# Half of a weight slab's load moved from SyncE's queue to ScalarE's, behind a dummy matmul

## The chip, the core and the metric

The kernel runs on one core of a Trainium2 chip. The core has five engines with queues of their own: TensorE (PE; its weight loads are listed as PEld), ScalarE (ACT), VectorE (DVE), GpSimd (POOL) and SyncE (SP). SP and ACT also issue DMAs, which move data between the chip's memory (HBM) and the core's SBUF. The metric is the device time of one execution in microseconds (us); lower is better.

## The reference

The kernel computes a two-layer block with a Silu between:

```
B, S, D, F = 1, 2048, 640, 1728
h = einsum("bsd,df->bsf", x, w1)
h = silu(h)
out = einsum("bsf,fd->bsd", h, w2)
```

All inputs and the output are bf16: x is 2048x640, w1 is 640x1728, w2 is 1728x640.

## The kernel before, in words

The first product is computed with the F dimension on the partitions. D is cut into five slices of 128 (the index k), F into 13 tiles of 128 (ft) and a rest of 64, S into four chunks of 512 (c). A matmul takes a 128x128 piece of w1 as weights and 512 columns of the transposed x as moving data, and five of them, one for each k, accumulate one tile of h in a PSUM bank. ACT applies Silu from the bank into `hT` (line 193). Then the second product runs from `hT` and `w2s`, results are copied out by DVE and ACT (lines 253 and 255), and SP stores them.

The first chunk's first eight ft tiles are computed in another order, so that PE can begin before all of w1 is there. `k_pass(k)` (lines 197 to 204) runs the eight matmuls of one k into eight banks, and five passes follow one another (lines 206 to 210). Pass k needs slab k, the 1024 columns of w1 that belong to k (256 KB, loaded by `load_k`, line 125), and two or one k slices of the transposed x (three DMA transposes, line 120, by `first(i)`: k 0 and 1, then 2 and 3, then 4). Slab 0 is loaded in two halves of 512 columns (128 KB): the first is needed by the matmuls of ft 0 to 3, the second by those of ft 4 to 7. Line 200 makes PE wait for the second half before ft 4.

The order of the DMAs is written out by hand, and a queue issues its DMAs one after another. The helper `ahead_of_start` puts an instruction ahead of the engine's part in the start barrier; `barrier_wait_here` moves an engine's wait for that barrier to the current place in its queue. The barrier opens when the Drain of each engine has been passed, and ACT, DVE, POOL and PE then go on. On SP, ahead of the Drain, stand: the transpose for k 0 and 1, the second half of slab 0 (line 149), slab 1, the transpose for k 2 and 3, slab 2 and slab 3. Behind it come the transpose for k 4, slab 4, the two groups of the other w1 columns (line 158), SP's wait for the barrier, the nine transposes of the other chunks and the loads of w2. On ACT, ahead of its Drain, stands the first half of slab 0 (line 147); behind the barrier come a wait for POOL's memset of `warm`, the load of the Silu table, one small activation (line 165) and then the Silus.

PE begins with 14 dummy matmuls on a zeroed tile `z` (128x256, line 183), which need only DVE's memset (line 138). They write bank 3, whose contents the first real matmul on it overwrites. Then come the passes, and PE's wait for the barrier stands after pass 1. `tick` attaches a semaphore increment to an instruction; `wait` makes an engine wait for a value, once.

Of the kernel before, what the change touches and what calls it, by code (L numbers as in the profile page):

```python
# [9 lines left out]
def bass_standalone__dense_activation_silu__prompt_kernel(  # L10
# [13 lines left out]
    P = 128  # L24
    NB = 8
# [5 lines left out]
    HB = 256  # L31
# [6 lines left out]
    pe, act, dve, pool, sp = nc.tensor, nc.scalar, nc.vector, nc.gpsimd, nc.sync  # L38

    with ExitStack() as es:  # L40
        def sb(name, shape, dtype):
            return es.enter_context(nc.sbuf_tensor(name, shape, dtype))

        xT = sb("xT", [P, DT, S], bf16)
        w1s = sb("w1s", [P, DT, F], bf16)
# [7 lines left out]
        z = sb("z", [P, HB], bf16)  # L53
        ps = es.enter_context(nc.psum_tensor("ps", [P, NB, BANK], fp32))
# [4 lines left out]
        def sem(name):  # L59
            s = es.enter_context(nc.semaphore(name))  # L60
            count[s.name if hasattr(s, "name") else name] = 0
            return [s, 0]

        def tick(ins, s, n=1):
            ins.then_inc(s[0], n)
            s[1] += n
            return (s, s[1])

        def wait(eng, *points):
            for pt in points:  # L70
                if pt is None:
                    continue
                s, v = pt
                key = (id(eng), id(s))
                if seen.get(key, 0) < v:
                    eng.wait_ge(s[0], v)
                    seen[key] = v

        s_pe, s_act, s_dve = sem("s_pe"), sem("s_act"), sem("s_dve")
# [4 lines left out]
        def load(eng, out_ap, in_ap):  # L84
            s = sem(f"s_ld{n_dma[0]}")
            n_dma[0] += 1
            return tick(eng.dma_start(out=out_ap, in_=in_ap), s, 16)

        ET = mybir.EngineType

        def preamble(engine, opcode):
            lst = nc.main_func.blocks[0].instructions
            return next(
                i for i, ins in enumerate(lst)
                if ins.opcode == opcode and ins.engine == engine
            )

        def ahead_of_start(emit, engine):
            lst = nc.main_func.blocks[0].instructions
            n = len(lst)  # L100
            r = emit()
            lst = nc.main_func.blocks[0].instructions
            new = lst[n:]
            del lst[n:]
            at = preamble(engine, "Drain")
            lst[at:at] = new
            return r

        def barrier_wait_here(engine):
            lst = nc.main_func.blocks[0].instructions  # L110
            lst.append(lst.pop(preamble(engine, "EventSemaphore")))

        w1_v = w1.rearrange("(dt p) f -> p dt f", p=P)
        w2_v = w2[0:F0, :].rearrange("(ft p) d -> p ft d", p=P)

        FA = 8
# [16 lines left out]
        def first(i):  # L133
            k0, k1 = KT[i]
            pt = turned(0, k0, k1, s_x[i])
            for k in range(k0, k1):
                ld_x[k] = pt
        p_z = ahead_of_start(lambda: tick(dve.memset(z[:, :], 0.0), s_dve), ET.DVE)  # L138
        FH = FA // 2
        ld_k = {}  # L140

        def slab(k):
            ld_k[k] = load_k(sp, k)

        ahead_of_start(lambda: first(0), ET.SP)
        ld_k0a = ahead_of_start(
            lambda: load(act, w1s[:, 0, 0:FH * P], w1_v[:, 0, 0:FH * P]), ET.Activation)
        ld_k[0] = ahead_of_start(
            lambda: load(sp, w1s[:, 0, FH * P:FA * P], w1_v[:, 0, FH * P:FA * P]), ET.SP)
        ahead_of_start(lambda: slab(1), ET.SP)  # L150
        ahead_of_start(lambda: first(1), ET.SP)
        ahead_of_start(lambda: slab(2), ET.SP)
# [3 lines left out]
        for a, b in FG:  # L156
            e = F if b == FT else b * P
            pt = load(sp, w1s[:, :, a * P:e], w1_v[:, :, a * P:e])
            for ft in range(a, b):
                ld_w1[ft] = pt  # L160
        barrier_wait_here(ET.SP)

        p_warm = tick(pool.memset(warm[:, :], 0.0), s_pool)  # L163
        wait(act, p_warm)
# [10 lines left out]
            load(sp, w2t[0:FL, :], w2[F0:F, :]),  # L175
            load(sp, w2t[FL:2 * FL, :], w2[F0:F, :]),
        ]

        bank_free = [None] * NB

        def dummies(n):
            for _ in range(n):
                pe.matmul(ps[:, 3, 0:HB], lhsT=z[:, 0:P], rhs=z[:, :], start=True, stop=True)  # L183

        wait(pe, p_z)
        dummies(14)

        def mm(o, l, r, start, stop, shared=False):
            return pe.matmul(o, lhsT=l, rhs=r, start=start, stop=stop, skip_group_check=shared)  # L189
# [7 lines left out]
        def k_pass(k):  # L197
            for ft in range(FA):
                if k == 0 and ft == FH:
                    wait(pe, ld_k[0])  # L200
# [19 lines left out]
        for ft in range(FA, FT):  # L220
            wait(pe, ld_w1[ft])
            b = bank()
            for k in range(DT):
                ins = mm(ps[:, b, :], w1s[:, k, ft * P:(ft + 1) * P], xT[:, k, 0:SCH],
                         start=(k == 0), stop=(k == DT - 1))
            silu(hT[:, ft, 0:SCH], ps[:, b, :], b, tick(ins, s_pe))
        for c in range(1, NSC):
            wait(pe, ld_xc[c])
            for ft in range(FT):
                b = bank()  # L230
                for k in range(DT):
                    ins = mm(ps[:, b, :], w1s[:, k, ft * P:(ft + 1) * P],
                             xT[:, k, c * SCH:(c + 1) * SCH], start=(k == 0), stop=(k == DT - 1))
                h_last = silu(hT[:, ft, c * SCH:(c + 1) * SCH], ps[:, b, :], b, tick(ins, s_pe))
        h_tail = []
        for q in range(NSC // 2):
            b = bank()
            for k in range(DT):
                for hh in range(2):
                    c = 2 * q + hh  # L240
                    ins = mm(ps[hh * FL:(hh + 1) * FL, b, :], w1s[:, k, F0:F],
                             xT[:, k, c * SCH:(c + 1) * SCH],
                             start=(k == 0), stop=(k == DT - 1), shared=True)
# [82 lines left out]
        for c in range(NSC):  # L326
            b = bank()
            wbank.append(b)
            for ft in range(FT):
                mm(ps[:, b, :], w2s[:, ft, DA:D], hT[:, ft, c * SCH:(c + 1) * SCH],  # L330
                   start=(ft == 0), stop=False)
# [51 lines left out]
```

## Time and profile before

| what | us |
|---|---|
| median of 5 runs | 124.95 |
| lowest and highest run | 124.69, 125.12 |
| the profiled execution | 124.77 |
| its span, first to last instruction | 123.4 |
| PE busy | 121.1 |
| ACT busy | 38.1 |
| DVE busy | 7.5 |
| the first half of slab 0 (ACT), issue to landing | 2.2 |
| the second half of slab 0 (SP), issue to landing | 3.2 |
| the transposes of x, median issue to landing | 4.0 |

The span starts with the first instruction that the profile has, SP's first transpose. In a line of the timeline the first number is the start, the second the duration, then come the engine, the line of the kernel, the operation and its tiles, and xN says how many instructions were merged. A q behind the engine's name marks its queue: a DMA's line there is the time of its issue, not of its transfer. Brackets give the idle time before it and what ended it. PEld overlaps PE, so an idle PEld is no loss in itself. Ends of matmuls are modelled; starts are what their pace is read from.

### The profile page before, as it was taken

Reading aid. Unit: us, or ns where it says so; the run is one execution under the profiler, and the core shown is the slowest. Engines: PE = TensorE matmul, PEld = TensorE weight load, DVE = VectorE, ACT = ScalarE, POOL = GpSimd, SP = SyncE. Lnnn points to the kernel's source line nnn. Section 1 sums busy time; section 2 is a strip of 40 time slices with the busy share of each in tenths; the row PEclk is TensorE's granted clock in tenths of the full one; section 3 lists DMA queues with packets and bytes.
Section 4 is the critical chain, followed back from the end, with each engine's and each line's share of the span. In section 5 each row is a group of like instructions: output and inputs, shape, how many; then the busy total and the mean of one; then the engine's idle time right before and its main releaser. Section 6 shows DMA issues by size and latency. Waiting matters only on the chain.

```text
span 123.4 us, 1342 instructions
## 1 busy us (share of the span) xinstructions
PE 121.1 (98%) x588; PEld 55.2 (45%) x588; DVE 7.5 (6%) x12; ACT 38.1 (31%) x66; POOL 0.3 (0%) x5
## 2 busy tenths in 40 slices
PE   8999999999999999999999999999999999999993
PEld 6344444444444444444434444444434443444452
DVE  0000000000000000000002020200022120102021
ACT  0313975555555555555430101010021101010100
POOL 0000000000000000000000000000000000000000
PEclk9999999999999999999999999999999999999999
DMA  5999899998000000000000000000003584111112
GB/s 139 246 281 305 186 185 119 154 367 328 5 0 0 0 5 0 3 0 0 0 0 0 5 0 0 0 0 0 0 0 85 90 305 173 53 53 53 53 62 98
DMA packets 19285, 10.35 MB, mean 84 GB/s; under 512 B 13264, under 2 KB 18768, under 8 KB 19280
## 3 DMA queue, kind: packets, MB, share of 16 engines
q1 hardware_dynamic: 19136, 10.15, 31.9%
q10 hardware_dynamic: 144, 0.13, 0.4%
q8 instruction: 4, 0.07, 0.2%
q14 instruction: 1, 0.01, 0.0%
HBM read 4.51 MB, written 2.62 MB: 58 GB/s over the span
## 4 chain that ended last, share of the span: by engine, by line
PE 98%; ACT 0%; issue 0%; DVEq 0%
PE ps L189 96%; PE ps L183 3%; ACT o_sb L255 0%; DVEq L368 0%
## 5 line engine op out<-in xcount | busy, mean ns | idle before, releaser
L189 PE MATMUL ps<-xT,w1s 128*128 128x512 bf16 (+1 forms) x280 | 59.1, 381 | 0.0
L189 PE MATMUL ps<-w2s,hT 128*128 128x512 bf16 (+2 forms) x221 | 45.4, 367 | 0.0
L189 PEld LDWEIGHTS ps<-xT,w1s 128*128 128x128 bf16 (+1 forms) x280 | 26.4, 99 | 32.6 <-issue 0.9
L193 ACT ACTIVATE hT<-ps 128x512 bf16<-128x512 f32 x52 | 30.0, 607 | 24.2 <-PE ps L189 24.2
L189 PEld LDWEIGHTS ps<-w2s,hT 128*128 128x128 bf16 x221 | 20.9, 98 | 24.4 <-issue 1.1
L255 ACT CAST o_sb<-ps 128x512 bf16<-128x512 f32 (+1 forms) x8 | 4.4, 546 | 42.2 <-PE ps L189 42.2
L253 DVE CAST o_sb<-ps 128x512 bf16<-128x512 f32 (+1 forms) x9 | 6.1, 677 | 100.0 <-PE ps L189 100.0
L189 PE MATMUL ps<-hT,w2s 128*128 128x512 bf16 x52 | 11.4, 379 | 0.0
L189 PEld LDWEIGHTS ps<-hT,w2s 128*128 128x128 bf16 x52 | 5.1, 98 | 6.1
L255 ACT CAST oT<-ps 128x512 bf16<-128x512 f32 x2 | 1.1, 588 | 11.0 <-PE ps L189 11.0
L183 PE MATMUL ps<-z 128*128 128x256 bf16 x14 | 3.2, 419 | 0.4 <-DVE z L138 0.4
L165 ACT ACT_TABLE_LOAD x1 | 1.3, 1283 | 5.2 <-DVEq L368 5.2
L183 PEld LDWEIGHTS ps<-z 128*128 128x128 bf16 x14 | 1.9, 145 | 1.1 <-DVE z L138 0.4
L189 PE MATMUL ps<-w2t,hTt 64*128 64x512 bf16 (+2 forms) x17 | 2.2, 366 | 0.0
L253 DVE CAST oT<-ps 128x512 bf16<-128x512 f32 x2 | 1.3, 686 | 13.7 <-PE ps L189 13.7
L193 ACT ACTIVATE hTt<-ps 128x512 bf16<-128x512 f32 x2 | 1.2, 598 | 1.1 <-PE ps L189 1.1
L189 PEld LDWEIGHTS ps<-w2t,hTt 64*128 64x128 bf16 x17 | 0.7, 94 | 1.4 <-issue 0.8
L189 PE MATMUL ps<-hTt,w2t 64*128 64x512 bf16 x4 | 0.6, 382 | 0.0
L189 PEld LDWEIGHTS ps<-hTt,w2t 64*128 64x128 bf16 x4 | 0.1, 94 | 0.4 <-issue 0.4
L165 ACT ACTIVATE warm<-warm 128x32 f32<-128x32 f32 x1 | 0.2, 229 | 0.0
L138 DVE MEMSET z<- 128x128 uint32 x1 | 0.2, 165 | 0.2 <-issue 0.2
L163 POOL MEMSET warm<- 128x32 f32 x1 | 0.1, 125 | 4.8 <-POOLq L368 4.8
(4 smaller groups left out, 0.4 us busy)
## 6 DMA issues: line engine op xcount, KB each, us to landing
out_dram<-o_sb SPq DMA_DIRECT2D x15, 160.0 KB, 1.9
w2s<-in_w_dram SPq DMA_DIRECT2D x1, 1120.0 KB, 6.6
w1s<-in_w_dram SPq DMA_DIRECT2D x4, 256.0 KB, 3.4
w2s<-in_w_dram SPq DMA_DIRECT2D x1, 960.0 KB, 8.7
w1s<-in_w_dram SPq DMA_DIRECT2D x1, 480.0 KB, 4.5
w1s<-in_w_dram SPq DMA_DIRECT2D x1, 400.0 KB, 5.2
xT<-in_x_dram SPq DMA_TRANSPOSE x12, 4.0
w2t<-in_w_dram SPq DMA_DIRECT2D x2, 80.0 KB, 8.1
```

What stands on the lines that cost most here:

```text
L138: p_z = ahead_of_start(lambda: tick(dve.memset(z[:, :], 0.0), s_dve), ET.DVE)
L163: p_warm = tick(pool.memset(warm[:, :], 0.0), s_pool)
L165: act.activation(out=warm[:, :], in_=warm[:, :], func=ACT.Silu)
L183: pe.matmul(ps[:, 3, 0:HB], lhsT=z[:, 0:P], rhs=z[:, :], start=True, stop=True)
L189: return pe.matmul(o, lhsT=l, rhs=r, start=start, stop=stop, skip_group_check=shared)
L193: r = tick(act.activation(out=out_ap, in_=in_ap, func=ACT.Silu), s_act)
L253: r = tick(dve.tensor_copy(out=out_ap, in_=in_ap), s_dve)
L255: r = tick(act.copy(out=out_ap, in_=in_ap), s_act)
```

## The change

The second half of slab 0 is no longer issued by SP between the first transpose and slab 1. ACT issues it, behind its own first half and its Drain, after a wait for a semaphore that the fourth of the 14 dummy matmuls increments; ACT's wait for the start barrier is moved behind this load. For that the dummies are written earlier in the program, as four and ten, and the last of each group increments `s_pe`. Their order on PE's queue is what it was.

```
+        bank_free = [None] * NB
+        def dummies(n):
+            for _ in range(n):
+                ins = pe.matmul(ps[:, 3, 0:HB], lhsT=z[:, 0:P], rhs=z[:, :], start=True, stop=True)
+            return tick(ins, s_pe)
+        wait(pe, p_z)
+        p_d0 = dummies(4)
+        dummies(10)
...
-        ld_k[0] = ahead_of_start(
-            lambda: load(sp, w1s[:, 0, FH * P:FA * P], w1_v[:, 0, FH * P:FA * P]), ET.SP)
...
         barrier_wait_here(ET.SP)
+        wait(act, p_d0)
+        ld_k[0] = load(act, w1s[:, 0, FH * P:FA * P], w1_v[:, 0, FH * P:FA * P])
+        barrier_wait_here(ET.Activation)
...
-        def dummies(n):
-            for _ in range(n):
-                pe.matmul(ps[:, 3, 0:HB], lhsT=z[:, 0:P], rhs=z[:, :], start=True, stop=True)
-        wait(pe, p_z)
-        dummies(14)
```

More of the change, by code (lines that the diff above doesn't have):

```diff
@@ L177, in bass_standalone__dense_activation_silu__prompt_kernel @@
         ]
-        bank_free = [None] * NB
-        def dummies(n):
-            for _ in range(n):
-                pe.matmul(ps[:, 3, 0:HB], lhsT=z[:, 0:P], rhs=z[:, :], start=True, stop=True)
-        wait(pe, p_z)
-        dummies(14)
         def mm(o, l, r, start, stop, shared=False):
```

## The prediction

> **What bounds the kernel now.** I read the page's list of busy times first, then the chain that ended last, then the timeline of the first eight microseconds, because the change touches nothing later. The two lines of the chain that carry nearly all of it:
>
> ```profile
> 0.39 3.17 PE ps L183 x14
> 3.56 117.93 PE ps L189 x573
> ```
>
> The reader is to see that from 0.39 us on TensorE (PE) follows only itself: 3.17 us of dummy matmuls, then 117.93 us of real ones. So the time can move in one way only: real matmuls start earlier or later, or a hole between them closes or opens. The timeline of the first eight microseconds shows what feeds them (start, duration, instruction; in brackets the idle time before it and what ended that):
>
> ```profile
> 0.00 1.35 SPq L120 DMA_TRANSPOSE xT<-in_x_dram  x1
> 0.12 0.38 ACTq L87 DMA_DIRECT2D w1s<-in_w_dram  x1
> ...
> 0.39 3.17 PE L183 MATMUL ps<-z 128*128 128x256 bf16 x14 [0.39 <-DVE z L138]
> 1.41 1.03 SPq L87 DMA_DIRECT2D w1s<-in_w_dram  x2
> 2.48 1.24 SPq L120 DMA_TRANSPOSE xT<-in_x_dram  x1
> 3.47 0.13 PEld L189 LDWEIGHTS ps<-xT,w1s 128*128 128x128 bf16 x2 [0.39 <-DMA xT<-in_x_dram]
> ...
> 3.77 1.05 SPq L87 DMA_DIRECT2D w1s<-in_w_dram  x2
> ...
> 4.62 2.38 PEld L189 LDWEIGHTS ps<-xT,w1s 128*128 128x128 bf16 x12 [0.21 <-DMA w1s<-in_w_dram]
> ...
> 7.39 0.56 PEld L189 LDWEIGHTS ps<-xT,w1s 128*128 128x128 bf16 x4 [0.39 <-issue]
> ```
>
> SP issues one DMA after another, and three weight loads (PEld) come late. The first, at 3.47, waits for the first transposed x; the second, at 4.62, for the half slab that the change moves; the third, at 7.39, starts the pass k=2. What the lateness costs PE is read from matmul starts. A group's last start is its start plus its duration less the 0.38 us of one matmul. In the window 4.6 to 6 eight matmuls stand as 4.30, 1.90: the last starts at 5.82, so seven steps take 1.52, **0.217 us a step**. The fourth real matmul starts at 4.53 (a group of four, 3.47 and 1.43), so the fifth, due at 4.74, needs its weights by about 4.62: the half slab (issued at 1.41, landed 3.2 later by the page's DMA list, at 4.6) comes just in time and costs PE nothing. At the third place two matmuls stand in a window as
>
> ```profile
> 7.12 0.68 PE L189 MATMUL ps<-xT,w1s 128*128 128x512 bf16 x2
> ```
>
> so the second starts at 7.42 where 7.12 + 0.217 = 7.33 was due: **a hole of 0.09 us**. Slab 2, issued at 3.77 and landed 3.5 later, at 7.27, made it. Slab 1 (2.02, landed 3.2 later, 5.2) is 0.2 ahead of its need near 5.4. No later hole in the trace is a DMA's.
>
> **The change, part by part.**
>
> *SP's queue.* Two copies take 1.03 from 1.41, of which the half slab alone is 0.56 (its line's durations) and slab 1 0.42. A copy right after a transpose takes 0.56 to 0.58, the next 0.42 to 0.43, so slab 1, now first, takes over the longer price. Slab 1 is issued at 1.41 instead of 2.02 (0.61 earlier); the second x transpose at 1.41 + 0.56 + 0.05 = 2.02 instead of 2.48 (**0.46 earlier**), and with it slabs 2 and 3, SP's drain, the start barrier, POOL's memset, the last x transpose, slab 4, the two w1 groups and the later x and w2 loads. The barrier holds ACT's table load and POOL's memset, both at 5.23; they move up to about 4.8, free, since ACT's first Silu comes at 11.29 after 4.54 us of idling.
>
> *ACT's queue.* ACT now waits for the fourth dummy. In the window around 1.0 three dummies stand as 0.58, 0.85; the last of them is the fourth and starts at 0.58 + 0.85 - 0.42 = 1.01, ending at 1.43. A hand-over costs some 0.03 us (DVE's last cast ends at 120.79 + 0.56 = 121.35, SP's store that waits for it starts at 121.37). So ACT issues at about 1.46, 0.05 later than SP did, for 0.38 as in its own line. Behind it on ACT stand the barrier wait, the table load, the warm-up and every Silu; they would have to slip over 4 us before PE felt it. Its signal for the barrier is given before the wait, so the others are not held. The dummies keep their order on PE, and two increments on matmuls add no instruction.
>
> *When the second half lands.* Unseen, so from both sides: ACT's own half landed 2.2 after its issue, which gives 3.7; SP's half took 3.2, which gives 4.7; and if slab 1, issued beside it, goes wholly ahead, 256 KB at the 353 GB/s moved from 6.20 to 7.20 add 0.74, up to 5.4. It is needed at 4.62. I take 4.2: a queue of its own does not stand behind the transpose, as SP's did, but shares with slab 1. Cost on the path: nothing taken, bounds 0 and 0.8.
>
> *When the first x lands.* It decides the first real matmul (issue at 0.00, landed 3.4 later). Now 128 KB can run beside its tail. The windows of the DMA's rate:
>
> ```profile
> 1.60:2.60 1.00, 1.00 (x7) 1.00 1.15 266
> 2.60:2.90 0.30, 0.30 (x3) 1.00 0.51 102
> 2.90:3.40 0.50, 0.50 (x4) 1.00 1.08 187
> ```
>
> (stretch, length, PE busy, granted clock, DMA share, GB/s). The transpose streams at 266 GB/s to about 2.6, and then the rate falls to 102. ACT's first half is issued at 0.12, and bytes move only after 1.0, so a half issued at 1.46 moves from about 2.4 on: mostly in that trough. If all of it went ahead of the transpose's tail, x would be 128 KB / 353 GB/s = 0.37 late. A delay there is half price: 13 dummy steps take 3.17 - 0.42 = 2.75, or 0.21 for 256 columns, against 0.217 for 512 later, so before about 4.3 PE runs at half rate (the clock column says 1.00 there, the steps say half). Bounds: nothing (no row shows how x could land earlier) and 0.37 / 2 = 0.19, or 0.37 should the fast clock slip as well. I take 0, since the half falls into the trough.
>
> *Pass k=2.* Slab 2 lands at 7.27 - 0.46 = 6.8 if landing follows issue, at 7.27 if the DMA engines are the limit. The trough and the 187 GB/s after it show room, so I take the former; only 0.09 is needed. **Gain 0.09**, bounds 0 and 0.09.
>
> *The runs.* The profiled execution took 124.77: the span of 123.4 and 1.37 around it. The median of the runs is 124.95, 0.18 more, and they scatter by 0.43. Three landings stand within 0.2 us of their need, so part of the 0.18 may be the same holes, larger; the change gives slabs 1 and 2 half a microsecond. An estimate between 0 and 0.18: I take 0.05.
>
> Sum: 124.77 - 0.09 = 124.68 for the profiled execution; on the median 124.95 - 0.09 - 0.05 = **124.8**.
>
> *A rule that speaks against it.* The Trainium skill, "DMA: Bandwidth & Descriptors", section "Issuing engines are not separate DMA queues", says that DMAs of all issuing engines end on the same 16 DMA engines, and that issuing from several saves only the sequencer's issue time. By it alone the change is worth SP's issue time at most and no bandwidth; the trough at 2.6, which a second queue might fill, would then stay, and the sum would lie between 124.8 and no change. Another page, "TensorE: Matmul & The Clock Gate", Part 1, has the clock released by a free-running window, at another moment from run to run; no run here shows that, and by it the 0.43 of scatter would be the clock's, out of this change's reach, and the sum 124.86.
>
> **The rivals.** A change can be told from none here beyond about 0.2%, 0.25 us: below 124.70 is faster, above 125.20 slower.
>
> 1. *Larger gain.* The median run loses more in the three tight places than the profiled one. All 0.18 and the 0.09 go, and some cold-clock time with them: 124.5 to 124.7. For it: the margins of 0, 0.2 and -0.09. Against: the profiled run, with its small hole, is itself at 124.77. 16 in 100.
> 2. *x is late.* The second half meets the transpose's tail: 0.1 to 0.37 late, at half to full price, on 124.86: 124.9 to 125.2. 14 in 100, 5 of them just beyond the bound.
> 3. *The half slab is late (the other side).* Place: the fifth real matmul, due at 4.74. ACT issues no earlier than SP did, and slab 1 now travels at the same time, not behind. Price: landing less 4.62, one for one, since the clock is full by then; with 5.4 that is 0.8, so 125.6. It decides from 0.4 late (124.81 + 0.4 = 125.2), a landing after 5.0. Against: SP's half, behind the transpose, landed at 4.6. 18 in 100: 125.2 to 125.6.
> 4. *It frees nothing.* The DMA engines are the limit and slab 2 lands as before; the hole stays: 124.9 to 125.0. 8 in 100.
>
> **How the numbers follow.** The forecast, hole closed and start kept, has 44 in 100, at 124.8, its own range 124.55 to 124.95; 14 of the 44 lie below 124.70. Faster: 14 + 16 = 30. Slower: 18 + 5 = 23. Within: 47. The range 124.5 to 125.3 leaves out most of rival 3 and a little of rival 1, some 17 in 100.
>
> **What would show it.** Right: ACT's second issue near 1.46, SP's second transpose near 2.0 and slab 2 near 3.3; the first real matmul still at 3.47; the step into k=2 at 0.22. Wrong: a weight load waiting for w1 at the fifth matmul well after 4.62 (rival 3), the first real load after 3.6 (rival 2), slab 2 landing still near 7.3 (rival 4).

## The result and the profile after

The changed kernel takes **125.46 us** (median of 43 runs, 125.01 to 126.06) where the kernel before takes 125.09 (median of 80 runs, 124.66 to 125.90; the 124.95 known ahead were five of these). The ratio is **1.0024, 95% interval 1.0015 to 1.0034**: slower by 0.37 us between the medians, by 0.30 going by the ratio. The forecast was 124.8, the range 124.5 to 125.3. Ratios leave out executions over 1.5% above the fastest of the same kernel: five of 12 of `e1_d1` and four of 10 of `e2_d8` (127.1 to 128.3), two of six of `e8_act_both` (129.0 and 129.6), none of the kernel before or the changed one.

The chain of waits of the changed kernel's first profile (125.48), its lines from SP's fourth DMA on:

```profile
3.29 4.74 DMA w1s<-in_w_dram
8.03 0.14 issue
8.16 114.06 PE ps L193 x557
```

In what follows, "the half" is the second half of slab 0, which the change moves, and a hole is time by which a matmul starts later than one step after the matmul ahead of it. The chain no longer starts with PE. It runs through a w1 transfer, slab 2, issued at 3.29 and landed 4.74 later, and PE's unbroken run begins at 8.16, at pass k=2. The same stretch of the timeline (start, duration, instruction, idle time before it) that was shown of the kernel before:

```profile
1.39 0.56 SPq L87 DMA_DIRECT2D w1s<-in_w_dram  x1
2.01 1.24 SPq L120 DMA_TRANSPOSE xT<-in_x_dram  x1
...
3.29 1.05 SPq L87 DMA_DIRECT2D w1s<-in_w_dram  x2
3.35 1.18 PE L193 MATMUL ps<-xT,w1s 128*128 128x512 bf16 x4
...
5.12 2.27 PEld L193 LDWEIGHTS ps<-xT,w1s 128*128 128x128 bf16 x12 [1.08 <-DMA w1s<-in_w_dram]
5.12 2.76 PE L193 MATMUL ps<-xT,w1s 128*128 128x512 bf16 x12 [0.59 <-DMA w1s<-in_w_dram]
...
8.16 1.02 PE L193 MATMUL ps<-xT,w1s 128*128 128x512 bf16 x4 [0.28 <-DMA w1s<-in_w_dram]
```

SP's issues are 0.5 to 0.6 us earlier. The first real matmul starts at 3.35, even earlier than the 3.47 of before. But the fifth, the first that needs the moved half, starts at 5.12 where 4.37 was due (the fourth starts at 3.35 + 1.18 - 0.38 = 4.15, plus 0.22). The idle time of 0.59 in brackets is less than the hole of 0.75 in the starts, since ends are modelled 0.16 beyond the step. Then pass k=2 starts at 8.16, where 7.51 + 0.22 = 7.73 was due: a second hole, of 0.43.

From that point nothing differs. In each profile of this study the execution's time less the start of the 17th real matmul (the first of pass k=2) is **117.3 us**: 124.77 - 7.42 before, 125.48 - 8.16 after. So for a profiled execution the whole question is when the 17th matmul starts. Two more profiles of the changed kernel and one of the kernel before (from the experiments) give the table; starts are read from narrow windows of the timeline, landings are the last semaphore increment of a DMA in the trace.

| profile | half of slab 0 lands | slab 1 | slab 2 | 5th matmul | 9th | 17th | time |
|---|---|---|---|---|---|---|---|
| before | 4.58 | 5.25 | 7.29 | 4.74 | 5.61 | 7.42 | 124.77 |
| before, second | 4.47 | 5.15 | 7.40 | 4.72 | 5.59 | 7.53 | 124.85 |
| after | 5.08 | 5.34 | 8.03 | 5.12 | 6.00 | 8.16 | 125.48 |
| after, second | 5.29 | 5.56 | 7.63 | 5.34 | 6.21 | 7.94 | 125.25 |
| after, third | 5.71 | 5.97 | 7.94 | 5.75 | 6.63 | 8.35 | 125.68 |

The half lands 0.5 to 1.2 us later than before and always within 0.3 us of slab 1, which itself is no earlier although it was issued 0.6 earlier. Two profiles of before are few: in the two of experiment 9, whose DMAs up to slab 2 are those of the kernel before, the half landed at 4.96 and 4.25. So the half ahead of slab 1 in one queue has 4.25 to 4.96 in four profiles, and the changed kernel's traffic 5.08 to 5.86 in five (with the two of experiment 6). One profile of the single queue lies at that edge, 5.10, with slab 2 moved ahead of the second transpose as well (experiment 4).

Only the first profile after has a hole at pass 2; in the other two the 17th matmul is the fifth plus twelve steps (5.75 + 12 x 0.2165 = 8.35). So two late landings compete. In the first profile slab 2 decides: the hole at the fifth matmul costs nothing more there, since PE would have waited for slab 2 in any case. In the other two the half decides. But slab 2 is later than before in all three. Where the 17th matmul waits for it, it starts 0.13 behind its landing (7.42, 7.53 and 8.16 in the table); by that, an estimate, slab 2 alone would have held it until 7.76 and 8.07 in the second and third profile, 0.2 to 0.65 later than before.

### The profile page after: what moved, and what is told of

Read it like the earlier page. It is cut to its first block, busy times and chain, and to the rows that moved or that the text cites. A ratio compares the mean times of both kernels' runs of the same rounds, so it can differ in the third digit from the quotient of the medians.

```text
span 124.2 us, 1342 instructions
## 1 busy us (share of the span) xinstructions
PE 121.0 (97%) x588; PEld 55.1 (44%) x588; DVE 7.5 (6%) x12; ACT 38.1 (31%) x66; POOL 0.3 (0%) x5
## 4 chain that ended last, share of the span: by engine, by line
PE 92%; DMA 4%; SPq 3%; issue 0%; ACT 0%
PE ps L193 92%; DMA w1s<-in_w_dram 4%; SPq L120 2%; SPq L87 0%; ACT o_sb L259 0%
```

## The experiments

Theories. A: the half, in a queue of its own, shares the DMA engines with slab 1, which now travels beside it. B: the half takes 3.6 us from its issue, whatever is beside it. C: the loss is slab 2's lateness at pass 2. Later ones: E, that a copy right in front of a transpose lands only with that transpose running; T, that the second x transpose holds the copies up; D, that a copy behind a transpose is slow by itself.

**1. The release moved.** The changed kernel with the half released by the first dummy, then by the eighth.

```
-        p_d0 = dummies(4)
-        dummies(10)
+        p_d0 = dummies(1)      # the other kernel: dummies(8)
+        dummies(13)            # the other kernel: dummies(6)
```

> ACT's second half is released by the first dummy matmul instead of the fourth, so issued near 0.8 us instead of 1.46. Theory A (sharing: in a queue of its own the half alternates with whatever SP's queue moves at that time; at 1.46 that is slab 1, and both land together at 5.1 to 5.3): now it meets the transpose instead, lands at 3.0 to 3.6, x lands up to 0.4 later than 3.16, no hole at the fifth real matmul, 0.3 to 0.5 us faster than the changed kernel. Theory B (the half just takes 3.6 us from its issue, whatever is beside it): lands at 4.4, hole under 0.1, x as in the changed kernel. Theory C (the time was lost at pass k=2 alone, where slab 2 landed at 8.03): no gain beyond 0.1.

Ratio 1.0021 (1.0003 to 1.0040): no gain on the kernel before, and none that can be told from the changed one. The profile, of an execution of 127.07, has the half at 4.35 and the first x at 4.53, where the changed kernel has x at 3.2 to 3.3; with PE starting that late it says nothing of the hole. Inconclusive on the landing; against the 0.3 to 0.5 us that A promised.

> Released by the eighth dummy, so issued near 2.3 us. Theory A: slab 1 goes mostly ahead, the half shares only its tail: lands at 5.1 to 5.5, hole 0.7 to 1.1, time 0 to 0.3 us over the changed kernel; slab 1 lands before 5.1. Theory B: lands 0.85 later than in the changed kernel, at 5.9, hole 1.5, 0.7 us over. Theory C: time as the changed kernel.

Ratio 1.0058 (1.0034 to 1.0083). The timeline around the hole:

```profile
2.31 0.35 ACTq L87 DMA_DIRECT2D w1s<-in_w_dram  x1
...
6.36 2.70 PEld L193 LDWEIGHTS ps<-xT,w1s 128*128 128x128 bf16 x14 [2.00 <-DMA w1s<-in_w_dram]
```

Issued 0.85 later, the half landed at 6.31, 1.23 later than in the changed kernel's first profile, and the fifth matmul waited until 6.36. Neither A (5.1 to 5.5) nor B (5.9) has that. Slab 1 was through by 5.07; what ran beside the half then was the second x transpose. C alone falls: the 17th matmul came at 8.96, twelve steps after the fifth, though slab 2 had landed at 7.89, so a wait at the fifth matmul can be paid in full.

**2. Slab 1 held, the half alone.** SP waits for the eighth dummy before slab 1.

```
-        ahead_of_start(lambda: slab(1), ET.SP)
+        ahead_of_start(lambda: (wait(sp, p_d1), slab(1)), ET.SP)   # p_d1: the eighth dummy
```

> The changed kernel, with slab 1 on SP's queue held until the eighth dummy (issue near 2.3 us instead of 1.39), so that the half has the DMA engines to itself behind the transpose. Theory A: the half lands at 3.7 to 4.3, no hole at the fifth matmul; slab 1 at 5.2 to 5.5 (a hole of 0 to 0.2 at pass 1), slab 2 and what follows on SP up to 0.5 later than before, hole at pass 2 of 0.3 to 0.6. Theory B: the half still lands near 5.1 and the hole of 0.75 stays.

Issues, the weight load of the fifth matmul, and the first matmul of pass 2:

```profile
1.46 0.35 ACTq L87 DMA_DIRECT2D w1s<-in_w_dram  x1
2.31 0.37 SPq L87 DMA_DIRECT2D w1s<-in_w_dram  x1
2.73 1.23 SPq L121 DMA_TRANSPOSE xT<-in_x_dram  x1
...
5.16 2.26 PEld L195 LDWEIGHTS ps<-xT,w1s 128*128 128x128 bf16 x11 [0.21 <-issue]
...
8.23 1.02 PE L195 MATMUL ps<-xT,w1s 128*128 128x512 bf16 x4 [0.32 <-DMA w1s<-in_w_dram]
```

From the same issue at 1.46 the half landed 2.8 us later, at 4.31 instead of 5.1 to 5.7, and the wait at the fifth matmul is gone (its load starts at 5.16 with no DMA in the brackets; PE was still at half rate there). **B falls.** Slab 1 landed at 5.29, as if it had been issued at 1.39. The queues of DMAs between 2.6 and 3.4 (packets, MB, share of the DMA engines' time; q10 is ACT's queue, q1 is SP's), first of the changed kernel, then with slab 1 held:

```profile
q1 hardware_dynamic: 68, 0.04, 36.1%
q10 hardware_dynamic: 34, 0.03, 32.8%
```

```profile
q10 hardware_dynamic: 100, 0.10, 62.1%
q1 hardware_dynamic: 233, 0.06, 38.4%
```

Both kernels issue the half at 1.46. Without slab 1 in SP's queue 0.10 MB of it move in this stretch, with it 0.03 MB, and the two queues together move less. So the half is not late only because a full rate is shared. Holding slab 1 also puts the second transpose 0.7 later; experiment 8 holds that one alone.

At pass 2, slab 2, now issued at 4.01, landed at 8.09, a hole of 0.48; the ratio is 1.0024 (1.0008 to 1.0040).

**3. No half at all.** The second half is left out of the start and loaded behind the other w1 loads; the last four matmuls of pass 0 use the first half's columns, so part of the first chunk's product is replaced.

```
-        wait(act, p_d0)
-        ld_k[0] = load(act, w1s[:, 0, FH * P:FA * P], w1_v[:, 0, FH * P:FA * P])
+        ld_k[0] = ld_k0a       # ft 4 to 7 of pass 0 read columns ft % FH; the half is loaded later, for chunk 1
```

> The second half of slab 0 is left out of the start: it is loaded last of the w1 loads on SP, and the four matmuls of pass 0 that need it use the columns of the first half. This is the most that SP's freed queue can be worth. Theory A: slab 1 lands at 4.3 to 4.7, slab 2 at 6.5 to 7.0, no hole at the fifth matmul nor at pass 2: 124.6 to 124.8 where the kernel before takes 125.0. Rival D (a copy behind a transpose is slow by itself): slab 1 lands at 5.0 or later even without the half beside it, and the time is not below that of the kernel before by more than 0.1.

Ratio 0.9983 (0.9965 to 1.0001). With 128 KB less beside it and the issue at 1.39, slab 1 landed at **5.08**, slab 2 at 7.44; the 17th matmul started at 7.58, 0.05 and 0.16 later than in the two profiles of before. So D holds for the landing, where my step needed it not to; its bound on the time, 0.1 us, does not (0.17% is 0.2 us). Even with the half gone, the freed issue time is worth 0.17%, not told from nothing, and 0.35% at the end of the interval. The rate of the DMA engines in the windows from 2.60 to 4.40 (columns as before: length, PE busy, clock, DMA share, GB/s), first after, then without the half:

```profile
2.60:2.90 0.30, 0.30 (x3) 1.00 0.74 121
2.90:3.40 0.50, 0.50 (x5) 1.00 0.66 70
3.40:4.40 1.00, 1.00 (x5) 1.00 0.91 312
```

```profile
2.60:2.90 0.30, 0.30 (x3) 1.00 1.59 169
2.90:3.40 0.50, 0.50 (x4) 1.00 0.63 99
3.40:4.40 1.00, 1.00 (x4) 1.00 1.09 249
```

The trough behind the first transpose, which I had counted as room, is not filled by a second queue once slab 1 has been issued at 1.39: 70 GB/s between 2.9 and 3.4 after, where the single queue had moved 187. It is there without the half too. With slab 1 held (experiment 2) it is room for the half: with x's tail 269 GB/s between 2.6 and 2.9, and 141 between 2.9 and 3.4. Why an issued slab 1 keeps it empty, no run here shows.

**4. Slab 2 ahead of the second transpose**, on the changed kernel and on the kernel before.

```
-        ahead_of_start(lambda: first(1), ET.SP)
         ahead_of_start(lambda: slab(2), ET.SP)
+        ahead_of_start(lambda: first(1), ET.SP)
```

> The changed kernel with slab 2 ahead of the second x transpose on SP's queue, so that copies and not a transpose follow slab 1. Theory E (a copy that lies right in front of a transpose, in whichever queue, lands only with that transpose running, near 5.1, however early it was issued): the half and slab 1 land engine by engine from 3.7 on, the half by 4.5, slab 1 by 4.9, no hole at the fifth matmul. Theory A (two queues alternate packet by packet, the half lands with the copies beside it): even more copies beside it, so the half lands at 5.1 or later and the hole stays at 0.7 or more. The second transpose lands later than 6.2, so a hole at pass 2 of any size up to 0.5 is left open by both.

> The kernel before with the same exchange of slab 2 and the second x transpose. Theory E: the half as before (3.7 to 4.6), slab 1 lands by 5.0, not in one burst at 5.2. If the exchange helps by itself, the time falls below 125.0; if the transpose then comes later than slab 2 did, the hole at pass 2 grows from 0.1 to 0.3 or more and the time is up to 0.3 over.

Changed kernel: the half landed at 5.30, its sixteen semaphore increments spread from 3.64 on, instead of within 0.2 us as in the first profile after. E does not follow from that: with the transpose behind the copies the half's increments are spread from 3.95 to 5.71 in the third profile after too, and E's forecast, a landing by 4.5, failed. With two slabs beside it the half is late, as A has it. Ratio 1.0021 (1.0002 to 1.0040). Kernel before: ratio 0.9985 (0.9964 to 1.0005), not told from no change; the half's last increment came at 5.10 there (the fifteenth at 4.43), which made a hole at the fifth matmul (5.15), and with slab 2 landed at 6.41 pass 2 had none.

**5. Second and third profiles.**

> The changed kernel unaltered, for a second profile. If the landing of the half at 5.1 is the mechanism and no accident, it lands at 4.9 to 5.3 again; the hole at the fifth matmul is 5.1 less what PE was ready at, so smaller (0 to 0.4) if the fast clock comes late. Theory C (slab 2's late landing was an accident of one run): hole at pass 2 near 0.1.

> The kernel before unaltered, for a second profile. If its first profile was typical, the half lands at 4.0 to 4.7 and the hole at pass 2 is 0.05 to 0.15; if that profile was a lucky one, slab 2 lands at 7.5 to 8.0 and the hole at pass 2 is 0.2 to 0.6, and the changed kernel's hole there is no loss of the change.

> The changed kernel unaltered, for a third profile and for the comparison on one chip: the half lands at 4.9 to 5.9, slab 1 at 5.3 to 6.1; ratio to the kernel before 1.001 to 1.004.

They are in the table above. The late half returns in each. So does slab 2's lateness (8.03, 7.63 and 7.94, against 7.29 and 7.40); what does not return is the hole at pass 2, since behind a late fifth matmul the 17th is due later. So C is no accident of one run and not the whole loss. The hole at pass 2 of the kernel before was 0.22 in its second profile. The third run's ratio is 1.0049 (1.0030 to 1.0069).

**6. The wait taken away, the traffic left.** Every DMA as in the changed kernel; the last four matmuls of pass 0 use the first half's columns (part of the first chunk's product is replaced), and PE waits for the half only at the second chunk. Run twice.

> The changed kernel with every DMA as it is, but the four matmuls of pass 0 that need the second half take the columns of the first half, and PE waits for the second half only at the second chunk. The traffic is the changed kernel's, the wait at the fifth matmul is gone. Theory A (the loss is that wait): the time goes back to that of the kernel before within 0.15, 0.2 to 0.4 under the changed kernel. Theory C (the loss is the slower traffic, through slab 2 at pass 2): the hole only moves to pass 2 (0.6 or more there) and the time stays that of the changed kernel.

> The changed kernel without the wait at the fifth matmul (pass 0 uses the first half's columns for the last four matmuls; every DMA as in the changed kernel), beside the changed kernel itself on one chip. If that wait is the loss: 0.2 to 0.5 us under the changed kernel. If slab 1 is as late as the half (5.3, 5.6 and 6.1 in three profiles, needed near 5.4), part of the loss stays at pass 1: 0.1 to 0.3 under.

Ratios 0.9985 (0.9966 to 1.0004) and 1.0047 (1.0030 to 1.0065): the two disagree. The kernel before, against which they are taken, had medians of 125.50 and 124.93 in the two comparisons, further apart than the loss in question. On one chip with the changed kernel the medians are 125.53 and 125.68, 0.15 apart (0.08 by the means), within the scatter of either. The first profile shows why so little can come back:

```profile
4.22 0.96 PEld L193 LDWEIGHTS ps<-xT,w1s 128*128 128x128 bf16 x5 [0.18 <-issue]
...
6.16 1.41 PEld L193 LDWEIGHTS ps<-xT,w1s 128*128 128x128 bf16 x8 [0.97 <-DMA w1s<-in_w_dram]
```

The fifth to eighth matmuls run on time, and the ninth waits until 6.16 for slab 1, which landed at 6.12. The wait moves on by one pass: the half and slab 1 are late together, so the loss is not the wait's alone. In the second profile no weight load after the first waits for a DMA: PE runs at half rate until 5.9, and the 17th matmul starts at 8.07, as late as in the changed kernel, for that reason.

**7. Slab 1 and the half on one queue, the transposes on the other.**

```
-        ahead_of_start(lambda: slab(1), ET.SP)
...
+        ld_k[1] = load_k(act, 1)       # behind the half on ACT
```

> The changed kernel with slab 1 also on ACT's queue, behind the half, so that one queue has the half ahead of slab 1; SP goes from the first x transpose straight to the second. Theory A (it is slab 1 beside it that delays the half): the half shares with the second transpose only, lands by 4.6, hole at the fifth matmul under 0.1. Rival Q (any work in the other queue delays it, of whatever kind, or ACT's queue is slow behind a transpose): the half lands at 5.0 or later and the hole stays. The second transpose lands at 4.5 to 5.5 instead of 6.2, slab 1 at 5.0 to 5.8, a hole of 0 to 0.5 at pass 1.

Ratio 1.0154 (1.0118 to 1.0190). The issues between 1.4 and 1.8, with their times to landing:

```profile
w1s<-in_w_dram ACTq DMA_DIRECT2D x1, 128.0 KB, 5.0
xT<-in_x_dram SPq DMA_TRANSPOSE x1, 7.8
```

The half landed at 6.42 and the second x transpose at 9.23 instead of 6.2. A falls in its narrow form, and rival Q holds: a transpose in the other queue went with a later half than slab 1 did.

**8. The second transpose alone held**, until the twelfth dummy; slab 1 and the half as in the changed kernel. Run twice.

```
-        ahead_of_start(lambda: first(1), ET.SP)
+        ahead_of_start(lambda: (wait(sp, p_d1), first(1)), ET.SP)   # p_d1: the twelfth dummy
```

> The changed kernel with the second x transpose (and all behind it on SP) held until the twelfth dummy, issue near 3.1 us instead of 2.0; the half and slab 1 are issued as in the changed kernel. Theory A (slab 1 beside it delays the half): slab 1 is still there, so the half lands at 4.8 or later. Theory T (the second transpose, whose bytes start at 4.2, holds both up before they have landed): with the transpose starting at 5 or later the half lands by 4.6 and slab 1 by 5.0, and the hole at the fifth matmul closes; pass 2 then waits 0.5 to 1.0 longer than in the changed kernel.

> The same kernel for a second profile: the landing of the half on the same side of 4.7 as in the first if the mechanism and not the run decides.

The first one's issues and the load of the fifth matmul:

```profile
1.41 0.56 SPq L87 DMA_DIRECT2D w1s<-in_w_dram  x1
1.46 0.35 ACTq L87 DMA_DIRECT2D w1s<-in_w_dram  x1
3.16 1.24 SPq L121 DMA_TRANSPOSE xT<-in_x_dram  x1
...
4.98 2.32 PEld L195 LDWEIGHTS ps<-xT,w1s 128*128 128x128 bf16 x12 [0.62 <-DMA w1s<-in_w_dram]
```

The half landed at 4.94 and 5.12, slab 1 at 5.11 and 5.32. So slab 1 beside it is enough to bring the half from 4.3 (experiment 2) to about 5.0, past its need of 4.6, as A has it. T's forecast (the half by 4.6, no hole) failed. The transpose may still add to the delay: the half landed at 5.08 to 5.86 in the five profiles with the changed kernel's traffic. With two profiles here and ranges that touch at 5.1, that part is likely and not shown. Holding the transpose costs at pass 2, where the holes are 1.05 and 0.37: ratio 1.0058 (1.0036 to 1.0080), where the changed kernel on the same chip had 1.0049.

**9. Slab 2 in two halves**, on the kernel before. This follows from the table: in its profiles slab 2 is what the 17th matmul waits for. Run twice.

```
-        ahead_of_start(lambda: slab(2), ET.SP)
+        ld_k2a = ahead_of_start(
+            lambda: load(sp, w1s[:, 2, 0:FH * P], w1_v[:, 2, 0:FH * P]), ET.SP)
+        ld_k[2] = ahead_of_start(
+            lambda: load(sp, w1s[:, 2, FH * P:FA * P], w1_v[:, 2, FH * P:FA * P]), ET.SP)
```

> The kernel before with slab 2 loaded in two halves as slab 0 is, so that pass 2 starts on the first of them. If the hole at pass 2 (0.09 and 0.22 us in two profiles of the kernel before) is slab 2's, it closes: 0.1 to 0.2 under the kernel before; if the second x transpose is as late, or the extra DMA pushes the rest back by 0.5, no gain.

> The kernel before with slab 2 in two halves, unaltered, to see whether its gain (ratio 0.9976 to the kernel before, interval 0.9955 to 0.9996) holds. If the split closes the hole at pass 2, the ratio is again 0.997 to 0.999 and the first half of slab 2 lands by 7.3; if the first measurement was scatter (the hole was still there in its profile, with the first half landing at 7.7), the ratio is 0.999 to 1.001.

Ratios 0.9976 (0.9955 to 0.9996) and 0.9987 (0.9963 to 1.0011). The first half of slab 2 landed at 7.71 and 6.99. Below the kernel before both times, beyond the interval only once, and that once in the comparison where the kernel before had its highest median (125.50, against 124.93 to 125.24 in the others): a candidate, not a proven gain; against the changed kernel's 1.0024 it is the better of the two.

## Why the prediction was wrong, step by step

*SP's and ACT's queues: right.* Slab 1 went out at 1.39 (1.41 forecast), the second transpose at 2.01 (2.02), ACT's half at 1.46 (1.46). What stands behind the waiting load on ACT cost nothing: behind the 17th matmul each profile takes the same 117.3.

*"When the second half lands ... I take 4.2 ... nothing taken": **the step that failed.*** It landed at 5.08, 5.29 and 5.71, the last beyond my upper bound of 5.4, and PE waited for it at the fifth matmul for 0.75, 0.28 and 1.15 us. I had argued that a queue of its own does not stand behind the transpose and that the trough at 2.6 to 2.9 was room. With slab 1 issued at 1.39 the trough is not room (experiments 2 and 3), and slab 1 beside it takes the half from 4.31 to about 5.0 (experiments 2 and 8). The second transpose, which I had not named as company at all, probably adds to it: a transpose in the other queue went with a landing at 6.42 in experiment 7, but no run shows its part in the changed kernel. What the kernel before had, the half ahead of slab 1 in one queue, I gave no worth.

The Trainium skill, "DMA: Bandwidth & Descriptors", section "Queues, rings and completion order", says that each DMA engine alternates between the queues that have work for it. The landings agree: in the first profile after, the half and slab 1 end 0.26 apart, though one is half the size. Between 3.4 and 4.4 ACT's queue moved 0.09 MB there and SP's 0.22 MB, in about the proportion of the two copies, so both come to their end together. The standstill before 3.4 is not explained by it.

*"Pass k=2": **wrong, and a second step that failed.*** I let slab 2's landing follow its issue, to 6.8. Issued some 0.47 earlier it landed at 8.03, 7.63 and 7.94, and at 7.44 with the half gone. The gain of 0.09 became a hole of 0.43 in the first profile, and in the others a loss that stands hidden behind the half's. Slab 1 landed at 5.07 (experiment 1, eighth dummy) and 5.08 (experiment 3) for an issue at 1.39, at 5.25 and 5.15 before for 2.02, and at 5.29 (experiment 2) for 2.31. The issue was not the limit, as rival 4 (8 in 100) had it, though slab 2 came later than there and the trough says that the DMA engines were not full all the time; and the rule on issuing engines that I had quoted against the change stood closer to the runs than my sum.

*"When the first x lands": right.* First real matmul at 3.35 in each profile after, 3.47 and 3.36 before. Rival 2 did not happen.

*Rival 3: its place and direction were right, its price half right.* It had 18 in 100, and the median falls in its 125.2 to 125.6. The hole at the fifth matmul is decided by the landing. "One for one, since the clock is full by then" is not: in the second profile after PE was still at half rate, the fifth matmul was due at 4.63 + 0.43 = 5.06 and the hole is 0.28. And in the first profile the hole of 0.75 is not the price, since slab 2 came later still.

*The runs.* The 0.18 between the profiled execution and the median need not be the tight places. In the second profile of experiment 9 the weight loads stand 0.43 apart until 6.34:

```profile
5.06 0.15 PEld L192 LDWEIGHTS ps<-xT,w1s 128*128 128x128 bf16 x1 [0.28 <-issue]
5.49 0.15 PEld L192 LDWEIGHTS ps<-xT,w1s 128*128 128x128 bf16 x1 [0.28 <-issue]
...
5.91 0.15 PEld L192 LDWEIGHTS ps<-xT,w1s 128*128 128x128 bf16 x1 [0.28 <-issue]
6.34 2.71 PEld L192 LDWEIGHTS ps<-xT,w1s 128*128 128x128 bf16 x13 [0.28 <-issue]
```

There PE runs at half rate until after 6.3, and its 17th matmul starts at 8.30 with no DMA late; the execution took 125.63. The kernel before has executions as long, up to 125.90, but none of them was profiled. The Trainium skill, "TensorE: Matmul & The Clock Gate", Part 1, has this as a clock released by a free-running window, some 0.5 us to either side of 4 us of activity. The profiles here agree in kind and go further: PE is busy from 0.39 on, and the full rate is there at 3.6 in the first profile of experiment 9 and only after 6.3 in the second. It also fits that the median lost 0.37 while the first profiles differ by 0.71: with a late full rate PE comes late to the fifth matmul by itself. This is argued from a few profiles, not shown by an experiment.

*The sum.* 125.46 less 124.8 is 0.66: 0.14 that the kernel before has over the median I started from, 0.14 of gains that did not come (0.09 and 0.05), 0.37 of loss, to rounding.

What stays open: why the queues move so little between 2.6 and 3.4 with slab 1 issued; whether and how the transpose holds up copies in the other queue; why slab 2 lands late (its fifteenth increment came at 7.52, 7.33 and 7.49, its last 0.3 to 0.5 behind, in the two profiles of before 0.06 and 0.11 behind); and how much of the median loss is the half, how much slab 1, slab 2 and the full rate, since experiment 6 gave two answers.

## What to carry to other kernels

When two loads that are needed one after the other go out in one queue, ask what their order is worth: here the first, moved to a second queue, landed with the second. Before counting freed issue time as a gain, look whether landings follow issues at all; here slab 1 landed at 5.1 for an issue at 1.39 (experiment 3) and at 5.3 for one at 2.31 (experiment 2). One hole in a timeline need not be the price: a later landing behind it can decide the time, as slab 2's did in the first profile. And reduce a comparison to the one event after which the traces are alike (here the 17th matmul): the time is then that event's start and a constant, and each landing gives a bound on the start.

## What the runs showed of the hardware that was not expected

- With copies in one queue and an x transpose in the other both were slow (experiment 7): the 128 KB copy took 5.0 us and the transpose 7.8, where the kernel before, with both in one queue, has 3.2 and 3.9. It is not always so: ACT's first half, issued 0.12 behind the first transpose, took 2.2.
- Behind the first x transpose the DMA engines move little for some 0.5 us once slab 1 has been issued, with one queue of copies or two: 99 and 70 GB/s between 2.9 and 3.4, against 250 to 310 in the following microsecond.
- The sixteen semaphore increments of a copy that a transpose follows in its queue mostly come together: slab 1's came within 0.10 to 0.26 us in eleven of thirteen profiles (0.66 and 1.02 in the other two), and over 1.17 and 1.27 us where slab 2 followed it (experiment 4).
- The full rate of TensorE came at moments from about 3.6 to 6.4 us under the same 14 dummies.
